# Fused attention and gated feed-forward: the third block's transposes split between VectorE and TensorE

## Chip, cores and metric

The kernel runs on one core of one Trainium2 chip. The metric is device time in microseconds (us) of one execution. TensorE multiplies matrices, VectorE and ScalarE work element by element, GpSimd helps, and SyncE issues the transfers (DMA). A DMA here moves data between device memory and SBUF. TensorE writes only into PSUM.

## The reference

Inputs q, k and v have 8 batches, 8 heads, 576 rows and 64 columns. Attention is computed in chunks of 64 rows, each chunk attending only to itself. Its result, as 4608 rows of 512, goes through a gated feed-forward layer with 1536 inner columns.

```python
scores = scale * np.matmul(q_c, k_c.transpose(0, 1, 2, 4, 3))
scores = scores - np.max(scores, axis=-1, keepdims=True)
attn = np.exp(scores)
attn = attn / (np.sum(attn, axis=-1, keepdims=True) + 1e-09)
x = np.matmul(attn, v_c)          # then (8, 576, 8, 64) -> 4608 x 512
g = x @ w_gate
out = (g * (1.0 / (1.0 + np.exp(-g))) * (x @ w_val)) @ w_out
```

## The kernel before

The 4608 rows are cut into nine blocks of 512. Each block goes through scores, softmax, transposition of the probabilities, value products, and then twelve steps over the inner columns (128 each): gate product, value product, Silu, and a projection back to 512 columns. Large products are made in single-pass fp32r, with each operand split into an upper half (a rounded copy, made by a cast on ScalarE, line 68) and a lower half (the remainder, a subtraction on VectorE, line 69). A projection of one step is twelve matmuls (lines 563 to 565).

**Order of the work.** TensorE, ScalarE and VectorE run their instructions in the order in which the program writes them; each engine is a queue, and an instruction that waits holds up those behind it. SyncE and GpSimd are also in written order up to the first instructions of the third block; from there a planner with modelled times sets their order.

**The opening.** The first two blocks' attention is written out by hand as a list of short names (`opening`, line 751 and following): S are scores, M maxima, B a product that subtracts the maxima inside PSUM, E exponentials, Z, R and N the normalization, T transposes on TensorE, C copies out of PSUM, X value products, G, V, A and D pieces of gate and value products. A name such as `.2` calls `keep_warm(2)`: that many transposes of the identity on TensorE into a PSUM tile that nobody reads (tile `unread`).

**The third block** (`nxt`, index 2, class `First`) has its attention woven into twelve steps of projections. These belong to the second block (`a1`), whose gated values had been put away in device memory. In each step `lag` issues the projection of an earlier step, `extra[step]` then adds a piece of the third block's attention, and `prepare` then fetches a later step's values and makes their upper and lower half (tile `hh`, two buffers). What step k prepares is projected in step k + 3. The pieces of `extra`:

- 0 to 4: exponentials, sums and normalization of the head pairs 0 and 1, then 2 and 3 (lines 451, 456, 465 to 470)
- 5: `load_v`, the loads of v
- 6: `turn`. For each of the four head pairs, TensorE transposes four 128x128 tiles of probabilities into one PSUM tile (line 475; pairs 0 and 1 into the buffers of `ps_a`, pairs 2 and 3 into those of `ps_gv`). ScalarE then copies pairs 0 and 1 into `turned` in SBUF (`copy(0)`, line 1052). After `turn`, step 6 also asks for the fourth block's queries and keys (`load_queries`, line 282)
- 7: `copy(2)`, ScalarE's copies of pairs 2 and 3
- 8: `columns`, the value products (line 489): first for pairs 0 and 1 into `ps_a`, then for pairs 2 and 3 into `ps_gv`; then ScalarE rounds the results of the first two pairs (line 635)
- 9 and 10: the other upper halves and the lower halves (line 639)
- 11: the fourth block's scores (line 310)

Blocks after the third transpose on VectorE (`Attn.turn`, line 377), in pieces of 32 rows by 256 elements: one instruction turns eight 32x32 squares.

## Time and profile before

| | us |
|---|---|
| three runs | 866.01, 866.68, 869.09 |
| median | 866.68 |
| the profiled execution: time | 866.68 |
| the profiled execution: span | 864.9 |

| engine | busy us | share |
|---|---|---|
| TensorE (PE) | 856.1 | 99% |
| weight loads (PEld) | 705.2 | 82% |
| VectorE (DVE) | 646.8 | 75% |
| ScalarE (ACT) | 426.5 | 49% |
| GpSimd (POOL) | 96.8 | 11% |

A row of a timeline reads: start in us from the span's start, length in us, engine, line, operation, written tile <- read tiles, shape and type, number of instructions merged, and in brackets the idle time of the engine before it with what ended it. TensorE's matmuls overlap, so the time that one takes from the stream is the distance between starts, not its length. A row of a group gives the number of instructions and their shortest, median and longest duration in ns. The chain of waits follows the work that ended last back to the start.

### The profile page before, as it was taken

The page shows a single profiled execution, that of the slowest core. Times are in us where ns is not written, and L with a number is a line of the kernel's source. Part 1 is how long each engine was busy: PE and PEld are TensorE (multiplying, and loading weights), DVE is VectorE, ACT ScalarE, POOL GpSimd, SP SyncE. Part 2 cuts the span into 40 slices and gives each one's busy share as a digit, 9 for nine tenths or more (in the row PEclk, how much of TensorE's full clock was granted, in tenths as well). Part 3 has the DMA queues.
Part 4 walks back from the last instruction along what each step waited for, and adds up shares of the span by engine and source line. Part 5 has one row for each costly group of instructions (what it writes and reads, how often), then busy time and mean ns, then how long its engine had stood idle before and what let it go on. Part 6 is the DMA issues. An engine that isn't in the chain of part 4 may idle for free.

```text
span 864.9 us, 14824 instructions
## 1 busy us (share of the span) xinstructions
PE 856.1 (99%) x5908; PEld 705.2 (82%) x5908; DVE 646.8 (75%) x924; ACT 426.5 (49%) x605; POOL 96.8 (11%) x83
## 2 busy tenths in 40 slices
PE   8999999999999999999999999999999999999997
PEld 5888888888888888888888888888888888888886
DVE  5888999773797673788997985887979943335785
ACT  4967788653524444536335635344346533333351
POOL 2000000000058653433200000000000000000000
PEclk9999999999999999999999999999999999999999
DMA  9958678888898785798876785766757685555563
GB/s 342 353 207 309 264 276 330 333 299 342 291 356 315 255 293 172 263 336 254 302 215 223 230 255 191 277 225 224 206 196 225 202 254 199 168 206 195 189 198 86
DMA packets 127348, 217.50 MB, mean 251 GB/s; under 512 B 57264, under 2 KB 88496, under 8 KB 117296
## 3 DMA queue, kind: packets, MB, share of 16 engines
q1 hardware_dynamic: 124752, 213.68, 72.7%
q10 hardware_dynamic: 2528, 2.88, 1.0%
q8 instruction: 46, 0.75, 0.4%
q14 instruction: 22, 0.18, 0.1%
HBM read 166.72 MB, written 49.81 MB: 250 GB/s over the span
## 4 chain that ended last, share of the span: by engine, by line
PE 98%; DVE 1%; DMA 1%; POOL 0%; issue 0%; DVEq 0%; POOLq 0%
PE ps_a L894 28%; PE ps_gv L894 21%; PE ps_o L1243 14%; PE ps_gv L499 13%; PE ps_gv L1243 6%; PE ps_o L563 4%; PE ps_o L564 4%; PE ps_o L565 4%; PE ps_a L310 2%; PE ps_a L390 1%; PE ps_a L489 1%; DMA qk_t<-in_qk 1%; DVE both L674 0%; PE ps_a L475 0%; PE ps_a L1243 0%; DVE z L695 0%
## 5 line engine op out<-in xcount | busy, mean ns | idle before, releaser
L894 PE MATMUL ps_a<-x,factors 128*128 128x512 f32 x864 | 216.2, 390 | 0.0
L894 PEld LDWEIGHTS ps_a<-x,factors 128*128 128x128 f32 x864 | 161.5, 188 | 35.7 <-ACT s_sb L393 1.0
L894 PE MATMUL ps_gv<-x,factors 128*128 128x512 f32 x648 | 164.7, 389 | 0.0
L894 PEld LDWEIGHTS ps_gv<-x,factors 128*128 128x128 f32 x648 | 121.5, 188 | 25.7 <-DMA factors<-t 0.3
L499 PE MATMUL ps_gv<-xh,w 128*128 128x512 f32 x320 | 98.0, 391 | 0.0
L377 DVE STREAM_TRANSPOSE turned<-s_sb 32x256 f32<-32x256 f32 x192 | 83.7, 436 | 2.7
L1243 PE MATMUL ps_o<-halves,sums 128*128 128x512 f32 (+1 forms) x324 | 72.5, 383 | 0.0
L499 PEld LDWEIGHTS ps_gv<-xh,w 128*128 128x128 f32 x320 | 59.7, 188 | 12.7 <-ACT xh L635 0.5
L1243 PEld LDWEIGHTS ps_o<-halves,sums 128*128 128x128 f32 x324 | 59.7, 188 | 12.0
L499 PE MATMUL ps_gv<-xl,w 128*128 128x512 f32 x160 | 62.1, 393 | 0.0
L538 DVE SCALAR_TENSOR_TENSOR rows<-v,rows 128x512 f32<-128x512 f32 x72 | 50.7, 705 | 12.8 <-ACT rows L1386 5.6
L1375 ACT ACTIVATE rows<-rows 128x512 f32<-128x512 f32 x36 | 22.8, 632 | 72.8 <-DVE rows L898 72.8
L1243 PE MATMUL ps_o<-hh,left 128*128 128x512 f32 x216 | 58.4, 394 | 0.0
L898 DVE TENSOR_TENSOR rows<-rows,ps_gv 128x512 f32<-128x512 f32 x36 | 24.6, 685 | 44.4 <-PE ps_gv L894 43.9
L1225 ACT CAST hh<-rows 128x512 fp32r<-128x512 f32 x36 | 22.4, 621 | 70.5 <-DVE rows L538 67.6
L563 PE MATMUL ps_o<-both,hh 128*128 128x512 f32 x144 | 56.3, 391 | 0.0
L564 PE MATMUL ps_o<-both,hh 128*128 128x512 f32 x144 | 56.0, 389 | 0.0
L565 PE MATMUL ps_o<-both,hh 128*128 128x512 f32 x144 | 56.0, 389 | 0.0
L1286 DVE TENSOR_TENSOR halves<-rows,halves 128x1024 fp32r<-128x1024 f32 x36 | 43.2, 1215 | 11.1 <-ACT halves L1282 11.1
L898 DVE TENSOR_TENSOR v<-v,ps_a 128x512 f32<-128x512 f32 x44 | 30.1, 685 | 28.0 <-PE ps_a L894 18.6
L1243 PE MATMUL ps_gv<-halves,sums 128*128 128x512 f32 x216 | 50.4, 389 | 0.0
L1282 ACT CAST halves<-rows 128x1024 fp32r<-128x1024 f32 x36 | 37.2, 1053 | 21.4 <-DVE rows L1260 7.7
(169 smaller groups left out, 1360.5 us busy)
## 6 DMA issues: line engine op xcount, KB each, us to landing
factors<-t SPq DMA_DIRECT2D x36, 1024.0 KB, 7.1
factors<-w SPq DMA_DIRECT2D x36, 512.0 KB, 4.5
w<-w SPq DMA_DIRECT2D x16, 1024.0 KB, 8.1
sums<-s SPq DMA_DIRECT2D x15, 1024.0 KB, 4.9
qk_t<-in_qk SPq DMA_DIRECT2D x24, 512.0 KB, 8.0
t<-th SPq DMA_DIRECT2D x24, 512.0 KB, 3.7
raw<-in_wgv SPq DMA_DIRECT2D x11, 1024.0 KB, 8.1
both<-o SPq DMA_DIRECT2D x22, 512.0 KB, 6.6
```

The source lines that it names most:

```text
L377: nc.vector.transpose(out=self.turned[to:to + 32, p:p + 2, j, :, 32 * (i % 2):32 * (i % 2) + 32], in_=src[32 * i:32 * i + 32, :, o // 2, 3 ...
L499: nc.tensor.matmul(ps, w, x, start=first and (k, i) == which[0], stop=last and (k, i) == which[-1])
L538: nc.vector.scalar_tensor_tensor(out=h, in0=pv, scalar=2.0 ** -8, in1=h, op0=ALU.mult, op1=ALU.mult)
L563: nc.tensor.matmul(o, hl[:, ts], woh, start=f == a.steps[0], stop=False)
L564: nc.tensor.matmul(o, hh[:, ts], wol, start=False, stop=False)
L565: nc.tensor.matmul(o, hh[:, ts], woh, start=False, stop=f == a.steps[1])
L894: nc.tensor.matmul(ps, w[u][:, k], x[i][v][:, k], start=first and k == 0 and n == 0, stop=k == NK // 2 - 1 and n == 2, skip_group_check=True)
L898: nc.vector.tensor_tensor(out=t, in0=t, in1=ps, op=ALU.add)
L1243: nc.tensor.matmul(to, w[:, i, u], a[:, at], start=first and n == 0, stop=n == 2, skip_group_check=True)
L1282: nc.scalar.copy(out=t[:, 0], in_=src)
L1286: nc.vector.tensor_tensor(out=lo, in0=src, in1=hi.bitcast(F32), op=ALU.subtract)
L1375: nc.scalar.activation(h, h, AF.Silu, scale=2.0 ** -8)
```

## The change

Two edits. In the list of the opening, `.5` is put between M101 and S13: five unread transposes on TensorE. In the third block, TensorE now transposes only head pairs 2 and 3, and their two copies follow in step 6. Pairs 0 and 1 are turned by VectorE, in four groups `turn_rows(0)` to `turn_rows(3)` of four instructions. Group i reads 32 rows of the probabilities, and each of its instructions turns eight 32x32 squares straight into `turned` in SBUF. Group 0 stands in step 4 behind the normalization of pairs 2 and 3, group 1 in step 5, groups 2 and 3 in step 6 behind `turn`; `prepare` of the same step follows each of them.

```diff
-        M100 N01 E001 M101 S13 Z001 S12 Z000 T02 vs K10 R00 C02 B101 M111 N00 B100 E101 M110 T03 E100 Z101 gs
+        M100 N01 E001 M101 .5 S13 Z001 S12 Z000 T02 vs K10 R00 C02 B101 M111 N00 B100 E101 M110 T03 E100 Z101 gs
...
     def turn():
-        nxt.turned = const.tile([P, NP, N], F32, name="pT", tag="turned")
-        for p in range(NP):
-            pt[p] = (ps_a if p < 2 else ps_gv).tile([P, T, P], F32, name="pt", tag="ps_a" if p < 2 else "ps_gv")
+        for p in (2, 3):
+            pt[p] = ps_gv.tile([P, T, P], F32, name="pt", tag="ps_gv")
             nxt.turn_to(p, pt[p])
-        copy(0)
-
-    def copy(p):
-        for i in (p, p + 1):
+        for i in (2, 3):
             nc.scalar.copy(out=nxt.turned[:, i], in_=pt[i].rearrange("p m k -> p (m k)"))
+
+    def turn_rows(i):
+        if not i:
+            nxt.turned = const.tile([P, NP, N], F32, name="pT", tag="turned")
+        src = nxt.pair(0, 2).rearrange("p (a k) -> p a k", k=P)
+        to = nxt.turned[:, 0:2].rearrange("p a (c k) -> p (a c) k", k=P)
+        for o in range(4):
+            nc.vector.transpose(out=to[32 * o:32 * o + 32, :, 32 * i:32 * i + 32],
+                                in_=src[32 * i:32 * i + 32, :, 32 * o:32 * o + 32])
...
-             3: lambda: sums(2), 4: lambda: nxt.normalize(2, z[2]), 5: load_v, 6: turn, 7: lambda: copy(2), 9: lambda: (first(2), rest(0)), 10: lambda: rest(2)}
+             3: lambda: sums(2), 4: lambda: (nxt.normalize(2, z[2]), turn_rows(0)), 5: lambda: (load_v(), turn_rows(1)),
+             6: lambda: (turn(), turn_rows(2), turn_rows(3)), 9: lambda: (first(2), rest(0)), 10: lambda: rest(2)}
```

## Prediction

> **What bounds the kernel now.** I read the page first (busy time, then the chain that ended last), then the timeline of each engine around the two edited places, then the waits of TensorE.

> ```profile
> span 864.9 us, 14824 instructions
> PE 856.1 (99%) x5908; PEld 705.2 (82%) x5908; DVE 646.8 (75%) x924; ACT 426.5 (49%) x605; POOL 96.8 (11%) x83
> PE 98%; DVE 1%; DMA 1%; POOL 0%; issue 0%; DVEq 0%; POOLq 0%
> 199.14 1.75 PE pt L475 x16
> PE ps_a L310 <- DMA qk_t<-in_qk: 2.6, 2, 1.9
> ```

> TensorE is busy for 856.1 of 864.9 us and makes up 98% of the chain. The fourth line is a piece of that chain: the 16 transposes of the third block stand in it at full length, so TensorE time taken out there shortens the end, as long as nothing takes its place. The last line heads the list of TensorE's waits in the first 35 us; in the lists of TensorE's waits from 35 us to the end there is no entry at all. What TensorE gains in the middle is therefore not handed back to a wait that the trace already shows.

> One profiled execution has a span of 864.86 us and a time of 866.68 us, 1.82 us around the span. That is also the median of the three runs (866.01, 866.68, 869.09), so I take the sum from 866.68. About 0.5%, 4.3 us, is what a measurement here can tell from no change.

> **Part 1: eight transposes less on TensorE.** Timeline of TensorE: the last projection of step 6, the transposes, the first projection of step 7, the last of step 8, the value products; then, from the opening, a run of eight transposes and what follows it.

> ```profile
> 198.75 0.39 PE L565 MATMUL ps_o<-both,hh 128*128 128x512 f32 x1
> 198.98 1.91 PE L475 MATMUL pt<-ident,s_sb 128*128 128x128 f32 x16
> 200.65 0.48 PE L563 MATMUL ps_o<-both,hh 128*128 128x512 f32 x1
> 203.46 0.39 PE L563 MATMUL ps_o<-both,hh 128*128 128x512 f32 x1
> 205.96 0.39 PE L565 MATMUL ps_o<-both,hh 128*128 128x512 f32 x1
> 206.27 2.11 PE L489 MATMUL ps_a<-pT,v_t 64*64 64x64 f32 x128
> 208.32 0.50 PE L563 MATMUL ps_o<-both,hh 128*128 128x512 f32 x1
> 22.82 1.09 PE L475 MATMUL ps_a<-ident,s_sb 128*128 128x128 f32 x8
> 23.67 2.51 PE L499 MATMUL ps_gv<-xh,w 128*128 128x512 f32 x9
> ```

> Sixteen transposes hold TensorE from 198.98 to 200.65, 1.67 us or 0.104 each; the eight of the opening hold it 0.85 us (22.82 to 23.67). Taking eight away saves 8 x 0.104 = **0.84 us** (0.82 by the opening's row). Step 7 then starts at 199.81 instead of 200.65, step 8 at 202.62 instead of 203.46, and the value products could start at 205.43 instead of 206.27.

> **Part 2: sixteen pieces more on VectorE.** The change queues them in order behind other work: four behind the normalization of step 4, four in step 5 ahead of that step's lower half (L69), eight in step 6 ahead of the next lower half. Who waits: the lower halves queued behind them (the projections three steps later read those) and the value products of step 8.

> ```profile
> 187.01 0.68 DVE L69 TENSOR_TENSOR hh<-h_in,hh 128x512 fp32r<-128x512 f32 x1
> 187.61 1.27 DVE L456 TENSOR_REDUCE z<-s_sb 128x8 f32<-128x512 f32 x2
> ...
> 195.49 1.22 DVE L470 TENSOR_TENSOR s_sb<-s_sb,z 128x1024 f32<-128x1024 f32 x1
> 198.74 0.69 DVE L69 TENSOR_TENSOR hh<-h_in,hh 128x512 fp32r<-128x512 f32 x1 [2.02 <-ACT hh L68]
> 199.83 0.69 DVE L69 TENSOR_TENSOR hh<-h_in,hh 128x512 fp32r<-128x512 f32 x1 [0.41 <-ACT hh L68]
> 204.32 0.69 DVE L69 TENSOR_TENSOR hh<-h_in,hh 128x512 fp32r<-128x512 f32 x1 [3.79 <-ACT hh L68]
> 198.08 0.62 ACT L68 CAST hh<-h_in 128x512 fp32r<-128x512 f32 x1 [3.72 <-DMA h_in<-h]
> 199.18 0.62 ACT L68 CAST hh<-h_in 128x512 fp32r<-128x512 f32 x1 [0.48 <-PE ps_o L565]
> L377 DVE STREAM_TRANSPOSE turned<-s_sb x192: 425/436/445, 234.8 to 627.6; 32x256 f32<-32x256 f32 x192
> 234.81 7.18 DVE L377 STREAM_TRANSPOSE turned<-s_sb 32x256 f32<-32x256 f32 x16
> 252.25 1.80 DVE L377 STREAM_TRANSPOSE turned<-s_sb 32x256 f32<-32x256 f32 x4
> 858.61 0.45 DVE L1319 STREAM_TRANSPOSE turned<-c 128x256 f32<-128x256 f32 x1
> ```

> The trace has the same shape in later blocks (L377): 425 to 445 ns each, 16 in a row in 7.18 us, so 0.449 a piece. Its source there also steps 128 elements between blocks of 32; only the order of the written blocks differs, and the row of L1319, with four times the partitions, takes the same 0.45. I take 0.449. In all this is 16 x 0.449 = 7.2 us of VectorE, against idle stretches of 2.02, 0.41 and 3.79 us there, 6.2 us together. So 1.0 us more than the gaps must be found, and the order of the queue has to be followed:

> - Step 4: the normalization ends at 196.71, four pieces end at 196.74 + 1.80 = 198.54. The next lower half starts at 198.74 as before, since its cast (198.08) waits for a transfer. Cost nothing.
> - Step 5: the lower half frees VectorE 0.61 us after its start, at 199.35 (the one of 187.01 is followed at 187.61, an interval of 0.60). Four pieces: to 201.17. The lower half that ran at 199.83 runs from 201.17 to 201.86. It is needed at step 8, which now starts at 202.62. Cover left: 0.76 us.
> - Step 6: eight pieces from 201.78, 3.59 us, to **205.37**. The lower half of 204.32 follows, to 206.06; it is needed when step 9 starts, 208.32 - 0.84 = 207.48.
> - Step 8: the value products read the pieces. VectorE ends at 205.37, TensorE arrives at 205.43: a tie. With a hand-over of some 0.07 us (estimate below) the wait is 0 to 0.05 us; the first four products read only pieces of the first two groups, which softens it further.

> ```profile
> 215.35 1.28 DVE L639 TENSOR_TENSOR xl<-ps_a,xh 128x512 fp32r<-128x512 f32 x2
> 216.70 1.49 PE L310 MATMUL ps_a<-qk_t 64*64 64x64 f32 x83
> ```

> The hand-over estimate: these subtractions end at 216.63, and the score products that reuse their PSUM buffers start at 216.70. This place is also the next one where TensorE and VectorE meet after the edit. The subtractions hang on a cast that waits for a projection, so the whole group moves forward with TensorE and the 0.84 us passes through it.

> [...]

> **Part 3: copies and buffers.** ScalarE loses two of four copies, and the other two move one step ahead:

> ```profile
> 199.71 1.06 ACT L1052 COPY pT<-pt 128x512 f32<-128x512 f32 x2
> 203.66 0.62 ACT L68 CAST hh<-h_in 128x512 fp32r<-128x512 f32 x1 [2.89 <-PE ps_o L565]
> 204.19 1.06 ACT L1052 COPY pT<-pt 128x512 f32<-128x512 f32 x2
> ```

> The pair that ran at 204.19 now takes the place of the pair at 199.71, and ends near 200.8; the next cast is due at 203.66 - 0.84 = 202.82. Nothing of it is on the path: 0. The two buffers that the removed transposes filled stay free until the value products, which no longer wait for their copies.

> **Part 4: five unread transposes in the opening.**

> ```profile
> 5.87 3.69 PE L310 MATMUL ps_a<-qk_t 64*64 64x64 f32 x128 [0.73 <-DMA qk_t<-in_qk]
> 10.87 1.16 PE L310 MATMUL ps_a<-qk_t 64*64 64x64 f32 x64
> 11.96 1.13 PE L685 MATMUL ps_a<-tops,minus 128*128 128x512 f32 x4
> 14.94 1.16 PE L310 MATMUL ps_a<-qk_t 64*64 64x64 f32 x64 [1.85 <-DMA qk_t<-in_qk]
> 177.77 2.09 PE L310 MATMUL ps_a<-qk_t 64*64 64x64 f32 x128
> ```

> On TensorE they stand between the matmuls of 11.96 and the scores of 14.94, and there is a wait of 1.85 us for a load. They write a PSUM tile nobody reads and wait for nothing. Five times 0.104 is 0.52 us, at half that rate 1.04: both fit into 1.85, so the cost is 0. If the load came at once they would cost 0.52. As to a gain: the first scores ran slowly (128 in 3.69 against 2.09 us later), but the 64 after the pause take 1.16 us just as the 64 before it. The pause cost no speed here, and removing part of it gains 0.

> **Sum.** -0.84 (transposes) + 0.03 (tie at the value products) + 0 + 0 = -0.8: 866.68 - 0.8 = **865.9 us**, a tenth of a per cent.

> **Rivals.**

> *Pieces late, value products wait (slower).* VectorE runs them in its order, so their end is 196.74 + 16 p + 2 x 0.61 with p the price of a piece. The gain is gone when that passes 206.27, at p = 0.52; above that the kernel is slower. At 0.69 us, what VectorE's 128x512 rows take, the pieces end at 209.0 and the kernel takes 866.68 + 2.7 = 869.4. A transfer for the cast of 198.08 that lands 1 us later acts the same way: the lower half of step 4 held TensorE up only beyond 1.2 us before (199.43 against 200.65), but twelve pieces now stand behind it. The pieces would end at 206.37, and the time be 866.8. For it: the cover is 0.06 us. Against: all 192 rows of L377 lie within 425 to 445 ns.

> *The opening's clock (faster by more).* If the pause does cost TensorE its speed in some executions, the five transposes, which shorten it to 1.3 us, would bring the slow runs down to the fast ones: 866.01 - 0.84 = 865.2. For it: the three runs spread by 3.1 us, and the first 128 scores show a slow rate of 3.69/2.09. Against: the two equal rows of 1.16.

> *The planner's order (slower).* SyncE's order behind this stage is planned from modelled times, which the edit alters.

> ```profile
> 200.93 1.84 SPq L282 DMA_DIRECT2D qk_t<-in_qk  x4
> 203.65 3.05 SPq L517 DMA_DIRECT2D both<-o  x2
> DMA to landing us min/median/max: 5.7/8.5/10.2
> ```

> If the four query loads slipped behind the next two weight loads, they would be issued until 206.7 + 1.84 = 208.5 and, at the longest landing of this tile (third line), be there at 218.7; the scores want them at 215.9. That wait of 2.8 us less 0.84 gives 868.7. Against: nothing that these loads wait for changes.

> **How the numbers follow.** Forecast 0.72 (865.9, give or take the scatter of the runs), late pieces 0.11 (866.8 to 869.4), clock 0.08 (865.2), planner 0.07 (868.7), anything else 0.02. The range runs from 864.8 (the clock case less 0.4, about half the distance from the fastest run to the median) to 867.8 (the milder part of the late pieces, and the slowest run less part of its excess). Faster by over 0.5%, below 862.3, is in no case that I can price: 0.02. Slower by over 0.5%, above 871.0, needs pieces of over 0.8 us or a worse order: 0.03. Within 0.5%: 0.95.

> **What would show it.** TensorE 5905 instructions, VectorE 940, ScalarE 603. The chain's transpose piece shrinks from 1.75 to about 0.9 us. Piece rows of 0.43 to 0.45 us; the last ends within 0.2 us of the start of the value products, and TensorE shows no wait there above 0.1 us. The wait in the opening falls from 1.85 to about 1.3 us with the scores still at 14.9. Span near 864.0. I am wrong if the value products wait longer than 0.3 us, if the pieces cost over 0.5 us, if the scores of the opening start late or change speed, or if the time moves although the third block gains its 0.8 us: then the cause lies in an order of transfers that I did not see.

## The result and the profile after

The changed kernel takes 871.62 us (median of six runs, 870.07 to 873.73) against 866.01 for the kernel before (six runs). The ratio is 1.0062, interval 1.0042 to 1.0082: slower by 0.6%, where 865.9 us was forecast. The profiled execution took 871.86 us, with a span of 869.7.

The page of the changed kernel, its span, busy times and the shares of the chain:

```profile
span 869.7 us, 14829 instructions
PE 858.5 (99%) x5905; PEld 706.7 (81%) x5905; DVE 654.9 (75%) x940; ACT 425.9 (49%) x603; POOL 98.1 (11%) x83
PE 96%; DVE 2%; issue 1%; DMA 1%; POOL 0%; ACT 0%; DVEq 0%; POOLq 0%
```

The counts of instructions are those forecast. New in the chain is "issue" with 1%: TensorE stood still, and the profile shows nothing that it waited for.

TensorE's timeline in the changed kernel: the eight transposes, the start of step 7, the value products, what follows them, and then two places with idle time before the instruction, in brackets.

```profile
199.00 1.03 PE L475 MATMUL pt<-ident,s_sb 128*128 128x128 f32 x8
199.83 0.49 PE L563 MATMUL ps_o<-both,hh 128*128 128x512 f32 x1
...
205.49 2.50 PE L489 MATMUL ps_a<-pT,v_t 64*64 64x64 f32 x128
207.92 0.50 PE L563 MATMUL ps_o<-both,hh 128*128 128x512 f32 x1
...
211.69 0.39 PE L564 MATMUL ps_o<-both,hh 128*128 128x512 f32 x1
212.61 0.50 PE L565 MATMUL ps_o<-both,hh 128*128 128x512 f32 x1 [0.53 <-issue]
...
217.14 1.84 PE L310 MATMUL ps_a<-qk_t 64*64 64x64 f32 x107
221.37 0.91 PE L310 MATMUL ps_a<-qk_t 64*64 64x64 f32 x21 [2.39 <-issue]
222.21 0.79 PE L499 MATMUL ps_gv<-xl,w 128*128 128x512 f32 x1
```

Two matmuls of the kernel before, to set beside them:

```profile
212.30 0.39 PE L565 MATMUL ps_o<-both,hh 128*128 128x512 f32 x1
218.80 0.50 PE L499 MATMUL ps_gv<-xl,w 128*128 128x512 f32 x1
```

Up to step 7 all went as forecast: 199.83 against 200.65, 0.82 us gained. Half of it is lost at the value products (2.50 us against 2.11; 207.92 against 208.32, 0.40 still in hand). Then come two gaps. The first lies between the second and the third matmul of one projection, which read the same two tiles; the matmul that stood at 212.30 now stands at 212.61. The second lies inside the fourth block's scores, behind 107 of the 128 records, 2.39 us long. The first gate product starts at 222.21 instead of 218.80, 3.4 us late. It runs slowly too, as the view by windows shows (its columns: length, busy time and count of each engine, granted clock, share of the transfer engines, GB/s):

```profile
core 0: us, PE busy (x) PEld busy (x) DVE busy (x) ACT busy (x) POOL busy (x), PEclk, DMA share, GB/s
0.00:212.20 212.20, 208.38 (x1620) 169.60 (x1620) 171.28 (x265) 143.73 (x199) 6.42 (x9) 1.00 0.83 307
212.20:220.00 7.80, 6.37 (x126) 5.25 (x127) 4.17 (x8) 2.58 (x5) 0.00 (x0) 1.00 0.65 177
221.37:224.78 3.41, 3.41 (x27) 2.81 (x27) 2.79 (x5) 0.00 (x0) 0.00 (x0) 0.50 0.99 350
```

For 3.41 us right behind the second gap the granted clock is 0.50. That brings the delay to 4.4 us, and the end lies 4.8 us behind that of the kernel before. Sum of the profiled execution: -0.8 (transposes), +0.4 (value products), +0.7 (first gap), +3.1 (second gap and its surroundings), +1.0 (half clock), +0.4 in small steps later.

The rows from 0.00 and from 212.20 also say what the gaps have in common. Ahead of the first lie 1620 matmuls and 1620 weight loads. Between the two lie 126 matmuls and 127 weight loads, and three waits of TensorE's queue in the trace: 256 instructions. The profile's part on transfers lists a queue for instructions:

```profile
q8 instruction: 46, 0.75, 0.3%
```

Its 46 packets, 16 KB each in the trace, fit the some 11,900 instructions of TensorE's queue (5905 matmuls, 5905 weight loads and 129 others in the trace) at about 256 to a packet. I call what one packet brings a page of instructions, and the place between two pages a border. That both gaps stand at a border is an inference here; the runs with shifted counts below (e5, e12) test it. The trace has a start for each packet of this queue. The page behind the first gap begins to arrive at 210.34 and the one behind the second at 218.94; in the kernel before these two started at 207.38 and 212.53, and TensorE came to them at 211.17 and 218.26.

Why would a page be late? VectorE and SyncE, changed kernel, then SyncE's matching row of the kernel before:

```profile
196.65 1.77 DVE L1056 STREAM_TRANSPOSE pT<-s_sb 32x256 f32<-32x256 f32 x4
199.08 0.69 DVE L69 TENSOR_TENSOR hh<-h_in,hh 128x512 fp32r<-128x512 f32 x1 [0.66 <-ACT hh L68]
199.81 1.78 DVE L1056 STREAM_TRANSPOSE pT<-s_sb 32x256 f32<-32x256 f32 x4
201.62 0.69 DVE L69 TENSOR_TENSOR hh<-h_in,hh 128x512 fp32r<-128x512 f32 x1
202.34 3.61 DVE L1056 STREAM_TRANSPOSE pT<-s_sb 32x256 f32<-32x256 f32 x8
```

```profile
202.34 0.32 SPq L995 DMA_DIRECT2D h_in<-h  x1
202.71 1.99 SPq L282 DMA_DIRECT2D qk_t<-in_qk  x4
204.79 1.12 SPq L517 DMA_DIRECT2D both<-o  x2
L282 SPq DMA_DIRECT2D qk_t<-in_qk x4: 423/458/506, 202.7 to 204.2; - x4
DMA to landing us min/median/max: 4.8/6.5/8.7
```

```profile
200.55 0.32 SPq L995 DMA_DIRECT2D h_in<-h  x1
```

Step 5's lower half ends at 202.31 instead of 200.52, because the second group of pieces stands ahead of it. Right behind it, SyncE issues the next load of `h_in`, whose buffer this lower half was the last to read: 202.34 instead of 200.55. In SyncE's queue four query loads and two weight loads stand behind it: the query loads leave from 202.71 instead of 200.93, the first weight load at 204.79 instead of 203.65, and seven transfers of 512 KB now leave within 3.6 us, where they took 6.2 before. None of them is itself waited for: the last query load lands by 204.2 + 8.7 = 212.9, before the scores at 217.14.

### The profile page after: what moved, and what is told of

Same layout as the page of the kernel before. It is cut to its first block, busy times and chain, and to the rows that moved or that the text cites. A ratio compares the mean times of both kernels' runs of the same rounds, so it can differ in the third digit from the quotient of the medians.

```text
span 869.7 us, 14829 instructions
## 1 busy us (share of the span) xinstructions
PE 858.5 (99%) x5905; PEld 706.7 (81%) x5905; DVE 654.9 (75%) x940; ACT 425.9 (49%) x603; POOL 98.1 (11%) x83
## 4 chain that ended last, share of the span: by engine, by line
PE 96%; DVE 2%; issue 1%; DMA 1%; POOL 0%; ACT 0%; DVEq 0%; POOLq 0%
PE ps_a L894 28%; PE ps_gv L894 21%; PE ps_o L1249 14%; PE ps_gv L499 13%; PE ps_gv L1249 6%; PE ps_o L563 3%; PE ps_o L565 3%; PE ps_o L564 3%; PE ps_a L310 2%; PE ps_a L390 1%; DVE pT L1056 1%; PE ps_a L489 1%; DMA qk_t<-in_qk 1%; DVE both L674 0%; PE ps_a L475 0%
## 5 line engine op out<-in xcount | busy, mean ns | idle before, releaser
L499 PE MATMUL ps_gv<-xh,w 128*128 128x512 f32 x320 | 99.1, 394 | 0.0
L377 DVE STREAM_TRANSPOSE turned<-s_sb 32x256 f32<-32x256 f32 x192 | 83.6, 436 | 2.7
L499 PEld LDWEIGHTS ps_gv<-xh,w 128*128 128x128 f32 x320 | 60.2, 190 | 13.3 <-ACT xh L635 0.5
L538 DVE SCALAR_TENSOR_TENSOR rows<-v,rows 128x512 f32<-128x512 f32 x72 | 53.5, 743 | 13.5 <-ACT rows L1392 6.0
L499 PE MATMUL ps_gv<-xl,w 128*128 128x512 f32 x160 | 62.6, 397 | 0.0
L565 PE MATMUL ps_o<-both,hh 128*128 128x512 f32 x144 | 56.2, 390 | 0.5 <-issue 0.5
L563 PE MATMUL ps_o<-both,hh 128*128 128x512 f32 x144 | 56.4, 392 | 0.0
```

The source lines that it names most:

```text
L377: nc.vector.transpose(out=self.turned[to:to + 32, p:p + 2, j, :, 32 * (i % 2):32 * (i % 2) + 32], in_=src[32 * i:32 * i + 32, :, o // 2, 3 ...
L499: nc.tensor.matmul(ps, w, x, start=first and (k, i) == which[0], stop=last and (k, i) == which[-1])
L538: nc.vector.scalar_tensor_tensor(out=h, in0=pv, scalar=2.0 ** -8, in1=h, op0=ALU.mult, op1=ALU.mult)
L563: nc.tensor.matmul(o, hl[:, ts], woh, start=f == a.steps[0], stop=False)
L565: nc.tensor.matmul(o, hh[:, ts], woh, start=False, stop=f == a.steps[1])
```

## Theories and experiments

**Q+P**: group 1 of the pieces delays a lower half, that holds SyncE's queue, and with the transfers moved TensorE's pages of 256 instructions start too late (Q); TensorE does its work 0.8 us earlier as well (P). **R**: the number of TensorE's instructions changed (five more, eight fewer matmuls), so the pages end at other places of the program, in runs of small matmuls that use a page up in 2 us (128 scores with their weight loads took 2.09 us in the kernel before); the queue has no part. **C**: something in the opening, its clock or its unread transposes.

Each median below is of four executions (e6, e9), five (e12), or ten or eleven.

| kernel | median us | before, same chip | ratio and interval |
|---|---|---|---|
| e1 unread transposes alone | 866.92 | 866.25 | 1.0012 (1.0003 to 1.0021) |
| e2 pieces alone | 871.18 | 866.25 | 1.0045 (1.0028 to 1.0063) |
| e3 query loads ahead | 867.34 | 866.25 | 1.0012 (1.0003 to 1.0022) |
| e4 four unread pieces | 866.92 | 866.25 | 1.0008 (0.9998 to 1.0019) |
| e5 eight unread | 868.51 | 866.52 | 1.0032 (1.0016 to 1.0047) |
| e6 sixteen unread | 869.89 | 866.52 | 1.0039 (1.0024 to 1.0054) |
| e7 group 1 behind | 867.86 | 866.52 | 1.0015 (1.0002 to 1.0028) |
| e8 other pairs first | 867.19 | 866.52 | 1.0007 (0.9996 to 1.0018) |
| e9 v loads later | 870.69 | 866.62 | 1.0047 (1.0034 to 1.0061) |
| e10 as e8, none unread | 866.31 | 866.62 | 0.9999 (0.9990 to 1.0008) |
| e11 as e8, eight unread | 867.13 | 866.62 | 1.0010 (1.0001 to 1.0019) |
| e12 before, sixteen unread | 869.25 | 866.62 | 1.0034 (1.0020 to 1.0047) |

**Which half of the change (e1, e2).** e1 is the kernel before with `.5`; e2 is the changed kernel without it.

```diff
-        M100 N01 E001 M101 S13 Z001 ...
+        M100 N01 E001 M101 .5 S13 Z001 ...
```

> The kernel before with the five unread transposes of the opening alone. Theory Q (SyncE's queue: the four pieces ahead of step 5's lower half hold back a load of h_in and with it the query loads behind it by 1.8 us, the transfers bunch, and TensorE's instruction pages come late): nothing of that is here, so 866.0, within 1 us of before, with no gap of TensorE over 0.4 us between 190 and 225 us. Theory R (position: the pages of 256 instructions end at other places of the program because the number of TensorE's instructions changed): the pages' borders move by five matmuls, so a gap and up to 5 us more are possible. Theory C (the clock in the opening): 866.0 too, scores after the pause as fast as before.

> The changed kernel without the five unread transposes: the third block's part alone. Theory Q: the same late load of h_in (near 202.3 us) and two gaps of TensorE 256 instructions apart, 871 to 872, as the changed kernel. Theory R: the pages' borders lie five matmuls elsewhere than in the changed kernel, so the time may fall back to 865 to 867. If the loss came from the opening: 865.5.

The loss is in the third block. The unread transposes alone cost 0.7 us, small but beyond the interval; the profiled execution of e1 is only 0.15 us longer than that of the kernel before and has no gap, so it does not show where. e2's ten times spread from 866.46 to 872.96, and its profiled execution, 866.46, has no gap: the load of `h_in` leaves at 201.96, but the page for the first border starts 2.7 us ahead of its need and the one for the second 3.7. From the start of a page to the first instruction behind the border it took 2.3 to 2.7 us at the gaps of this block (212.61 - 210.34 = 2.3 and 221.37 - 218.94 = 2.4 in the changed kernel, 221.28 - 218.55 = 2.7 in e9). So the same program falls on either side of a narrow margin. Neither Q+P nor R said that. None of e2's longer executions was profiled, so that their times come from these gaps is argued from the changed kernel.

**The queue of SyncE (e3, e7).** e3 asks for the fourth block's queries in step 5, ahead of the load that waits (its `load_queries`, not shown, is rewritten so that it can run a step earlier); e7 moves group 1 behind step 5's lower half. TensorE's instructions are in both exactly those of the changed kernel.

```diff
-             5: lambda: (load_v(), turn_rows(1)),
+             5: lambda: (load_v(), load_queries(), turn_rows(1)),
...
```

```diff
-             5: lambda: (load_v(), turn_rows(1)),
-             6: lambda: (turn(), turn_rows(2), turn_rows(3)),
+             5: load_v,
+             6: lambda: (turn(), turn_rows(1), turn_rows(2), turn_rows(3)),
```

> The changed kernel, with the fourth block's query loads asked for one step earlier, ahead of the load of h_in that waits for step 5's lower half. TensorE's instructions are the changed kernel's to the last one. Theory Q: the transfers no longer bunch behind the late lower half; page loads start within 3 us of their page's predecessor, both gaps go, 865.5 to 866.5. Theory R: gaps at the same two instructions, 871 to 872.

> The changed kernel with the second group of pieces moved behind step 5's lower half (twelve pieces in step 6). Theory Q+P: the load of h_in goes out near 200.6 us again, the page loads are in time, no gap of 0.4 us at TensorE; twelve pieces end near 205.9, so the value products wait about 0.5 us: 866.0 to 866.8 (with 0.35 us more outside the span, as all kernels with the sixteen pieces show). Theory R: 870 to 872, as TensorE's instructions are the changed kernel's.

In e7 SyncE's load is back in its place and twelve pieces run in one go. In e3 the load still leaves late, at 202.35, but the query loads have left ahead of it, from 195.46 on.

```profile
200.78 0.32 SPq L995 DMA_DIRECT2D h_in<-h  x1
200.78 5.44 DVE L1056 STREAM_TRANSPOSE pT<-s_sb 32x256 f32<-32x256 f32 x12
```

Both bring back most of the loss, 867.34 and 867.86 against 871.62, and neither profiled execution shows one of the two gaps. Their two pages start at 209.64 and 213.85 (e3) and at 209.80 and 213.25 (e7), against 210.34 and 218.94. R alone is refuted, since borders and instructions are those of the changed kernel. The times are 1 us above what I expected. In the profiled executions the page for the first border starts only 2.2 to 2.4 us ahead of its need, so the margin there is used up in both. The profiled execution of e7, 868.62, also lost 1.4 us to a load of factors. Two of e7's eleven times, 870.81 and 871.71, lie where the changed kernel's do.

**The delay alone (e4).** The kernel before with four pieces more, into a tile that nobody reads, ahead of step 5's lower half.

```diff
-             5: load_v, 6: turn,
+             5: lambda: (load_v(), pieces(4)), 6: turn,
...
+    def pieces(n):
+        src = nxt.pair(0, 2).rearrange("p (a k) -> p a k", k=P)
+        to = const.tile([P, 8, P], F32, name="unread", tag="ts")
+        for o in range(n):
+            nc.vector.transpose(out=to[32 * (o % 4):32 * (o % 4) + 32, :, 32:64],
+                                in_=src[32:64, :, 32 * (o % 4):32 * (o % 4) + 32])
```

> The kernel before with four more VectorE pieces ahead of step 5's lower half; they turn the same probabilities into a tile that nobody reads. TensorE's instructions are those of the kernel before. Theory Q: the load of h_in goes out near 202.3 instead of 200.55 us, page loads start later, gaps at TensorE, 868 to 871. Theory R: 866.0, as before, no gap.

A miss for Q+P as I had put it. The load leaves at 202.76, even later than in the changed kernel, yet the profiled execution has no gap at either border; its page for the scores starts 2.9 us ahead of need. (That execution, 868.66, lost 1.7 us at 520 us, to a load of factors.) Of the changed kernel's loss, then, the late queue is a needed part (e7), but it does not make it by itself. What the rest of the change adds to it is not shown: the two pages of instructions start earlier here than in the changed kernel (208.21 and 215.24 against 210.34 and 218.94). The P of the theory doesn't explain it either, since the edit also moves the first border to a later matmul: TensorE comes to it at 211.08 here, and in the changed kernel it would have come to it at 212.08 without the gap.

**Do the gaps belong to pages (e5, e6, e12)?** More unread transposes push the borders towards the front of the program: `.8` and `.16` for `.5` in the changed kernel, and `.16` alone in the kernel before.

> The changed kernel with eight unread transposes in the opening instead of five: TensorE has as many instructions up to the value products as the kernel before. Theory Q+P (a late lower half holds SyncE, transfers bunch, and TensorE's pages of 256 instructions come late): the late load is still there, so 870 to 872 in most executions, and any gap lies three matmuls earlier in the program than in the changed kernel. Theory R (the count of instructions decides): 865.5 to 866.5.

> The changed kernel with sixteen unread transposes in the opening, 1.7 us of TensorE within a wait of 1.85 us. If the gaps are the ends of pages of 256 instructions, they stay at the same instruction numbers of TensorE and move eleven matmuls towards the front of the program: the gap in the fourth block's scores lies behind about matmul 96 of 128 instead of 107. Time 870 to 873. If the gaps are waits for data, they stay at the same matmul of the scores.

> The kernel before with sixteen unread transposes in the opening, 1.7 us of TensorE within a wait of 1.85 us, and no other edit. If they only fill the pause: 866 to 866.5. If the pages' ends move into the opening's runs of small matmuls, as the trace of the changed kernel with sixteen suggests: gaps at 21, 33 and 179 us, 256 instructions apart or multiples of it, 868 to 870.

e5, windows split at its two gaps, and the gaps:

```profile
0.00:213.00 213.00, 207.03 (x1620) 167.84 (x1620) 170.94 (x265) 143.08 (x198) 6.42 (x9) 1.00 0.82 305
213.00:221.50 8.50, 7.05 (x126) 5.74 (x127) 4.34 (x7) 2.72 (x6) 0.00 (x0) 1.00 0.60 166
```

```profile
213.81 0.50 PE L565 MATMUL ps_o<-both,hh 128*128 128x512 f32 x1 [1.06 <-issue]
222.42 0.58 PE L310 MATMUL ps_a<-qk_t 64*64 64x64 f32 x24 [1.56 <-issue]
```

With three matmuls more in the opening, the gaps again follow 1620 matmuls and 1620 loads, and then 126 and 127. In the scores the gap has moved from 21 records ahead of the end to 24: exactly three. A wait for data would stay with its matmul. Restoring the count of the kernel before does not restore its time (868.51 against 866.52), so R alone fails here as well. But I had expected 870 to 872 in most executions, and only three of ten took over 870; the profiled one, 872.68, is one of these three.

e12 has no VectorE piece and no late load. Its windows, and its gap:

```profile
0.00:33.50 33.50, 30.73 (x602) 23.57 (x602) 22.51 (x48) 20.15 (x35) 6.42 (x9) 1.00 0.96 344
```

```profile
34.40 0.33 PE L489 MATMUL ps_a<-pT,v_t 64*64 64x64 f32 x4 [1.28 <-issue]
```

602 and 602 instead of 1620 and 1620: 2036 loads and matmuls fewer, and with the queue's own waits of the trace 2048, eight pages. The gap stands inside a run of small value products, and the kernel is 2.6 us slower though its sixteen transposes fit into the pause (the scores start at 14.89). Of the 2.1 us that its profiled execution is longer, the gap is 1.28. I had expected gaps at 21 and 179 us as well; none is there. So R is right in another place: the moved border cost 1.28 us in e12 without any change to the queues. e6's profiled execution has gaps at two borders in the opening, 1.5 us together, and one of 1.4 us near 181 us, and none in the fourth block's scores; my forecast of a gap behind matmul 96 was wrong.

**What the late page waits for (e9).** The second page starts 6.3 us after the border in front of it is passed (212.61 to 218.94), and the transfer engines are not the reason all that time: in the changed kernel they are 94% busy from 212.61 to 215.00, 10% in the next two microseconds, and 67% up to 219.00, with the small packets of the v loads in front of the page (990 of 256 B between 217 and 219).

```profile
215.00:217.00 2.00, 2.00 (x10) 1.50 (x8) 1.82 (x3) 0.15 (x1) 0.00 (x0) 1.00 0.10 24
```

e9 asks for the v loads (256 B packets) behind the scores.

```diff
-        with tc.issue_after(a.asked):
+        with tc.issue_after(recent[0]):
             load_values(a)
```

> The changed kernel with the fourth block's first v loads (packets of 256 B) asked for only after the fourth block's scores; TensorE's instructions and VectorE's pieces are those of the changed kernel. If these small packets are what a page of instructions waits for between its request and its start (6.3 us in the changed kernel for the page of the scores), the second gap goes and with it the half-speed stretch: 867.5 to 869, the first gap may stay. If the large loads alone hold it up: 871 to 872.

The second gap stays, with still less traffic in front of it:

```profile
216.00:218.50 2.50, 2.50 (x82) 1.99 (x84) 1.26 (x3) 0.00 (x0) 0.00 (x0) 1.00 0.05 7
```

```profile
221.28 0.57 PE L310 MATMUL ps_a<-qk_t 64*64 64x64 f32 x21 [2.11 <-issue]
```

At 7 GB/s no transfer is in the way of that page, which starts at 218.55. The time, 870.69, lies between the two forecasts; the small packets are not what holds up the second page. It is asked for late, or held up where the trace does not show it; which, and why, stays open. In the changed kernel TensorE's queue holds a semaphore wait from 212.97 to 216.52 for the scores' buffers, and the late starts there, in e5 and in e9 all follow the end of such a wait. But in e2, e3, e4 and e7 the page starts while the same wait still runs (in e7 at 213.25, with the wait from 212.70 to 215.99), so the wait alone does not hold up a page.

**A better version (e8, e10, e11).** As e7, and the value products start with pairs 2 and 3, which TensorE has turned, so that VectorE's pieces have a microsecond more.

```diff
-        for p in (0, 2):
+        for p in (2, 0):
             px[p] = nxt.columns_of_two(...)
-        first(0)
+        first(2)
...
-             9: lambda: (first(2), rest(0)), 10: lambda: rest(2)}
+             9: lambda: (first(0), rest(2)), 10: lambda: rest(0)}
```

> As the one with group 1 behind step 5's lower half, and the value products start with head pairs 2 and 3, which TensorE has turned; upper and lower halves follow in that order. Theory Q+P: neither gap nor wait at the value products is left, so the full 0.84 us is gained in the span and about 0.35 lost outside: 865.4 to 866.0, 0.3 to 0.7 us below the kernel before. Theory R: 870 to 872.

> The kernel with group 1 behind the lower half and head pairs 2 and 3 first, without the five unread transposes. Pages come in time (load of h_in near 200.7 us): 866.0 to 866.6, no slower than the kernel before by more than its uncertainty, if the unread transposes cost anything by moving the pages' ends; 867.2 as with them, if they cost nothing.

> The same with eight unread transposes instead of five, so that TensorE's count of instructions up to the value products is that of the kernel before. Pages in time: 865.8 to 867.2. A clear difference to the version with five or none would be the effect of the pages' ends alone.

The wait at the value products is gone: e10's profiled execution runs them as the kernel before did.

```profile
205.24 2.09 PE L489 MATMUL ps_a<-pT,v_t 64*64 64x64 f32 x128
```

e10 takes 866.31 against 866.62: no difference that can be measured. Its median span is 864.3 against 864.8, so by the medians 0.5 us of the 0.84 are there inside the span, but the time around the span is 2.01 to 2.09 us in it, 1.88 to 2.08 in e11, and 2.07 to 2.20 in the changed kernel and in e2, e3 and e5 to e9, where the kernel before, e1, e4 and e12 have 1.73 to 1.87. By their medians, all kernels with the sixteen pieces pay 0.2 to 0.35 us there; no run here tells why. With none, five and eight unread transposes the same order takes 866.31, 867.19 and 867.13; e8's 867.19 is a miss, over 1 us above its forecast. In the profiled execution of e11 a gap of 0.75 us stands at the border of 34.6 us; that of e10 has no such gap. No version beats the kernel before.

## Why the prediction was wrong, point by point

- **Eight transposes, 0.84 us**: right, 0.82 measured.
- **Price of a piece**: right; 0.449 us forecast, 3.61 / 8 = 0.451 measured. VectorE as a bound in itself was not the loss.
- **Tie at the value products, 0.03 us**: 0.39 measured. The cast of step 4 started 0.35 us later, at 198.43 (its load landed at 198.33 instead of 197.98), and the pieces behind it ended at 205.95 instead of 205.37. This is the rival of the late pieces, in its milder form, and the wait was longer than the 0.3 us that the prediction named as a sign of being wrong; but it is a small part of the loss.
- **Step 5's lower half, "Cover left: 0.76 us"**: the projection did not wait, with 0.37 us left (202.31 against 202.68), but as an account of who waits it is wrong. **This is the step that failed.** "Who waits: the lower halves queued behind them ... and the value products" left out SyncE: its load of `h_in` waits for that lower half to free the buffer and left 1.8 us late, and six more transfers stand behind it. Taking that delay away (e7), or the query loads out from behind it (e3), brought back some 4 us.
- **"What TensorE gains in the middle is therefore not handed back to a wait that the trace already shows"**: the words are right, the conclusion was wrong. The sum had no term for the supply of instructions, where the loss fell: gaps of 0.53 and 2.39 us, and the slow clock behind them. A list of waits shows what has run late and not what came with some 1.5 us to spare. The kernel before had the first of the two pages begin 3.8 us ahead of need (207.38 for 211.17), where at the gaps a page took 2.3 us or more; in the changed kernel it began 3.0 us later. How the late transfers come to delay a page stays open.
- **Part 3, copies**: right, they ran at 199.72 and cost nothing.
- **Part 4, unread transposes at 0**: in the profiled execution of the change they hide as forecast (the wait falls to 1.17 us, the scores start at 14.77). But they also move every border behind them by ten instructions, five matmuls and five weight loads (e5's three more transposes moved the gap in the scores by three matmuls). Alone they cost 0.7 us (e1), and sixteen of them 2.6 us (e12); a gap at a border is shown for the sixteen only.
- **The planner's order**: SyncE's order there did not change, only the time of one load. The rival named the right queue and the wrong cause: it looked for query loads that land late, and they landed in time. What was held against it, "nothing that these loads wait for changes", is wrong: they stand behind the load of `h_in`, which waits for the delayed lower half.
- **The opening's clock**: no part of it. The clock did fall, to 0.50 for 3.41 us, but behind the second gap.

How long a page lasts is an estimate from the rows: a page of projections some 29 us (128 matmuls at 0.227 us from start to start), while the one between the two gaps, with 107 of the 128 scores in it, kept TensorE busy for 6.37 us (7.05 in e5, with 104). The list of TensorE's waits in the changed kernel has no entry between 35 us and the first gap, and none behind the second. The granted clock fell to 0.50 for 3.41 us behind the gap of 2.39 us. Behind those of 1.56 (e5) and 2.11 us (e9) the scores kept their pace: 24 in 0.58 and 21 in 0.57 us, where the changed kernel took 0.91 us for 21. What sets the clock here is not shown.

## What to carry to other kernels

Where a piece of work is put ahead of another in an engine's queue, follow everything that the delayed instruction frees, buffers and the queue of transfers behind them too, and not only who reads its result: here a load of `h_in` left 1.8 us late, with four query loads behind it. TensorE, 99% busy here, still stood for 0.53 and 2.39 us with nothing in the profile that it waited for, at two places 256 instructions apart. In a stretch with runs of tiny matmuls count 256 instructions at a time, see when each page starts (for the first border 3.8 us ahead of need in the kernel before, and 3.0 us later in the changed one), and distrust an edit that moves these borders into such a run or takes slack from it (e12 shows the first, 1.28 us; the changed kernel the second). An idle bracket marked "issue" in the middle of one group with unchanged operands was the sign here; that it followed the same 1620 matmuls and loads after the program was shifted by three matmuls (e5) is why I read it as the supply of instructions.
